# Three moves in a layer of attention and feed-forward, and the scheduler's timeline model for all engines but TensorE

## The chip, the cores and the metric

One core of a Trainium2 chip. The metric is the device time of one execution, in microseconds (us). The engines are called as in the profile: PE is TensorE (PEld its weight loads), DVE VectorE, ACT ScalarE, POOL GpSimd, and SP SyncE, which issues nearly all of the DMAs here.

## The reference

S = 2048 tokens, D = 512, F = 1792; 32 heads of 16; a causal window of 256 tokens. Everything is float32.

```python
def _A_ref(x, wqkv, wo):
    qkv = ...(x @ wqkv).reshape(B, S, 3, H, Dh)...
    q, k, v = qkv[0], qkv[1], qkv[2]
    scores = jnp.einsum("bhqd,bhkd->bhqk", q, k) * (Dh ** -0.5)
    mask = (idx[:, None] - idx[None, :] >= 0) & (idx[:, None] - idx[None, :] < W)
    p = _softmax(jnp.where(mask[None, None], scores, -1e9), axis=-1)
    return ...jnp.einsum("bhqk,bhkd->bhqd", p, v)... @ wo

def _B_ref(x, w1, w3, w2):
    h = _silu(jnp.einsum("bsd,df->bsf", x, w1)) * jnp.einsum("bsd,df->bsf", x, w3)
    return jnp.einsum("bsf,fd->bsd", h, w2)

xn = _layernorm(x, axis=-1)
return x + _A_ref(xn, A_wqkv, A_wo) * _silu(_B_ref(xn, B_w1, B_w3, B_w2))
```

## The kernel before

**Numbers.** Dense products are computed from float16 pairs: an operand is cut into a high half (a cast) and a low half (a subtraction), and a product is three matmuls, high by high, high by low and low by high. That is why so many of the casts and subtractions exist: for each 128x512 operand a cast (mostly on ACT) and one or two subtractions on GpSimd. Weights are also measured (`squares`, L239 on ACT and L241 on DVE, and `measure_down`, L886) and scaled by a power of two before they are cut (`split_pool`, L332, L333 on ACT, L329 on GpSimd).

**Tiles and units.** The tokens are worked in four tiles (t = 0 to 3) of 512. Of attention there are 32 units: four tiles, four groups of eight heads (g), two halves of a group (p). A unit runs `pass1` (scores L650 and their row maxima L664) and `pass2` (scores L730, masks L737, exponentials L740, values L758). Between the batches of a unit `spread` puts pieces of dense work: the projections to Q, K and V (`project`, matmuls L583, evictions L599 on ACT and L603 on DVE; `value`, L553 and L556), the gate and up products (`gate_up`, matmuls L991; tanh L1006 on ACT; product L1010 and L1015 on DVE), the down product, and the outputs (`residual` L1207 and `total` L1222 to L1237).

**Q and K go through DRAM.** They are stored transposed (L606 to L610) to `dQ` and `dK` and read back in another layout as `qa` and `KA` (`fetch`, L626). The reciprocal of the softmax's sums goes through DRAM too (`normalise`: read `dr`, invert it at L799, store and spread it).

**Weights.** Tile 0 loads the raw float32 weights, measures and cuts them. The cut halves of wqkv, w1 and w3 are stored to DRAM (`dWQ` L589, `dW1` L997), and tiles 1 to 3 load them from there (L617, L832). Loads for tile 0 are issued at L384 (wqkv), L836 (w1, w3) and L877 (w2).

**The fold of w2.** Tile 0 multiplies by w2 as it is (L1184). For tiles 1 to 3 the down product is done block by block in seven products in place of eight. That takes sums of blocks of w2, made once, in tile 1's time, by `fold_weights` for seven pairs of blocks: load the raw pair e, o (L943), scale it (ACT, L949), make the sums z and y (GpSimd, L951 to L954), then cut e, o, z and y (`cut`: a cast at L959 on ACT, subtractions at L961 on GpSimd), and store them to `dW2` (L966). On the other side, `fold_first` and `fold_second` make the sums of the hidden activations (GpSimd L1078 to L1081) and cut them (ACT L1053 and L1069; GpSimd L1054, L1072, L1073). `load_fold` (L1095) brings w2's halves back, `fold_down_piece` multiplies (L1114; evictions L1128 on ACT and L1132 on DVE), and `unfold` (L1148) adds the seven results.

**What sets the order.** PE runs in the order in which the program is written (`ORDERED` holds TensorE alone). The instructions of DVE, ACT, GpSimd and SP are ordered by the framework's scheduler, with `urgent()` (a higher priority) around evictions, and `tc.issue_after(x)`, which holds an instruction back behind x. The program's own clock is a count of steps: `later(n, f)` writes f's instructions n steps on. Nearly all operands live in 55 slots of one pool. `give(slot, after=n)` offers a slot for reuse from n steps on; `take` picks the slot that was free earliest:

```python
    def give(*tiles, after=0):
        for made in tiles:
            given[0] += 1
            free.append((now[0] + after, given[0], held.pop(id(made))[0]))
```

An instruction that writes to a reused slot waits for the last reader of what was in it.

Of the kernel before, what the change touches and what calls it, by code (L numbers as in the profile page):

```python
# [21 lines left out]
P = 128  # L22
S = 2048
D = 512
# [22 lines left out]
KR = TERMS * DH  # L47
# [6 lines left out]
ORDERED = {ENGINE.PE}  # L54
# [28 lines left out]
def tile_block(ctx: ExitStack, tc: tile.TileContext, x, wqkv, wo, w1, w3, w2, out):  # L83
# [142 lines left out]
    dW1 = dram.tile([FB, 2, P, 2 * NC * P], F16, name="dW1")  # L226
    dW2 = dram.tile([7, P, FB // 2, D], F16, name="dW2")


    def squares(parts, on_act=0, apart=0):  # L230

# [335 lines left out]
    def project(t, g, k, terms=(range(3),), scores_bank=False):  # L567


        cell = {}  # L570

        parts = ([[(c, i) for c in (2 * half, 2 * half + 1) for i in range(3)] for half in range(2)] if len(terms) == 1
                 else [[(c, i) for i in group for c in range(NC)] for group in terms])

        def part(n):
            assert turned[t] == 4
            w = WQ[t, g, k]
            xh, xl = X[t]
            if n == 0:
                cell["pp"] = pss.tile([P, 2, TW], F32, name="s")[:, 0, :] if scores_bank else bank([P, TW])  # L580
            for c, i in parts[n]:
                a, b = ((0, xh), (1, xh), (0, xl))[i]
                nc.tensor.matmul(cell["pp"], w[:, (a * NC + c) * P:(a * NC + c + 1) * P], b[:, c, :], start=(c, i) == parts[0][0],  # L583
                                 stop=(c, i) == parts[-1][-1])
            if n < len(parts) - 1:
                return
            if t == 0:
                def store():
                    nc.sync.dma_start(dWQ[g, k], w)  # L589
                    give(w, after=4)  # L590
                later(8, store)
            else:
                give(w)
            pp = cell["pp"]
            both = take(F16)
            B = both.rearrange("p (a t) -> p a t", a=2)
            s = QS / (XS * WS)
            with urgent():
                nc.scalar.activation(B[:, 0, :], pp, AF.Copy, scale=s)  # L599

            def rest():
                with urgent():
                    lasts["emptied"] = nc.vector.scalar_tensor_tensor(B[:, 1, :], pp, s, B[:, 0, :], op0=ALU.mult, op1=ALU.subtract)  # L603
                d = (dQ, dK)[k][g][:, :, t * TW:(t + 1) * TW]
                if k == 0:
                    nc.sync.dma_start(d[:, 0:2, :], B[:, 0:1, :].to_broadcast([P, 2, TW]))  # L606
                    nc.sync.dma_start(d[:, 2, :], B[:, 1, :])
                else:
                    nc.sync.dma_start(d[:, 0:2, :], B)
                    nc.sync.dma_start(d[:, 2, :], B[:, 0, :])  # L610
                give(both, after=4)
            later(1, rest)
        return opening([(len(l), lambda n=n: part(n)) for n, l in enumerate(parts)])
# [5 lines left out]
    def fetch(t, g):  # L619
        QA[t, g] = qa = qpool.tile([P, 4, TW], F16, name="qa")  # L620
        ka = keys(t, g)
        c0 = 0 if t else 2 * P
        for dst, d in ((ka[:, :, c0:], dK[g][:, :, t * TW - 2 * P + c0:(t + 1) * TW]),
                       (qa, dQ[g][:, :, t * TW:(t + 1) * TW])):
            for r in range(2):
                nc.sync.dma_start(dst[64 * r:64 * r + KR],  # L626
                                  d[64 * r:64 * r + 64].rearrange("(a d) i t -> (d i) a t", d=DH))


# [197 lines left out]
    def load(t, f):  # L827
        if t:
            a = [take(F16) for _ in range(2)]
            WF[t, f] = [a, None]  # L830
            for k in range(2):
                nc.sync.dma_start(a[k], dW1[f, k])  # L832
            return
        RAW[f] = raw = [take(F32) for _ in range(2)]
        for k, w in enumerate((w1, w3)):
            nc.sync.dma_start(raw[k].rearrange("p (c f) -> p c f", f=P),  # L836
                              w[:, f * P:(f + 1) * P].rearrange("(c p) f -> p c f", p=P))

    measured = set()
# [34 lines left out]

    def load_down(f):
        RAW2[f] = raw = take(F32)
        nc.sync.dma_start(raw, w2[f * P:(f + 1) * P, :])  # L877

    def measure_down(k, f):

# [53 lines left out]
    def fold_weights(j):  # L934

        cell = {}
        l, r = slice(0, 256), slice(256, 512)
        sub = nc.gpsimd.tensor_sub

        def load():  # L940
            cell["raw"] = [take(F32) for _ in range(2)]
            for i, raw in enumerate(cell["raw"]):
                nc.sync.dma_start(raw, w2[(2 * j + i) * P:(2 * j + i + 1) * P, :])  # L943

        def sums():
            assert folded
            e, o = cell["raw"]
            for i, raw in enumerate((e, o)):
                nc.scalar.activation(raw, raw, AF.Copy, scale=fold_w[:, 2 * j + i:2 * j + i + 1])  # L949
            cell["z"] = z, y = [take(F32) for _ in range(2)]  # L950
            sub(z[:, l], e[:, r], e[:, l])  # L951
            sub(z[:, r], o[:, r], z[:, l])
            sub(y[:, l], o[:, r], e[:, r])
            sub(y[:, r], o[:, l], z[:, r])  # L954

        def cut(raw, n, which):

            a = take(F16)
            nc.scalar.copy(a[:, 0:n], raw[:, 0:n])  # L959
            for c in range(0, n, 256):  # L960
                sub(a[:, n + c:n + c + 256], raw[:, c:c + 256], a[:, c:c + 256])  # L961
            give(raw, after=6)

            def store():
                for c, i in enumerate(which):
                    nc.sync.dma_start(dW2[i, :, j, :].rearrange("p (h d) -> p h d", h=2),  # L966
                                      a[:, 0:2 * n].rearrange("p (h c d) -> p c h d", h=2, d=256)[:, c])
                give(a, after=4)
            later(4, store)

        def cuts():
            e, o = cell["raw"]
            z, y = cell["z"]
            for n, work in enumerate(((e, 256, (0,)), (o, 512, (1, 2)), (z, 512, (4, 5)), (y, 512, (6, 3)))):
                later(2 * n, lambda work=work: cut(*work))
        return load, sums, cuts
# [3 lines left out]
    def gate_up(t, f):  # L980
        cell = {}

        def part(k, half):
# [10 lines left out]
                return  # L994
            if t == 0:
                def store():
                    nc.sync.dma_start(dW1[f, k], w)  # L997
                    give(w, after=4)
                later(8, store)
            else:  # L1000
                give(w)
            if k == 0:
                cell["s"] = sg = take(F32)

                with urgent():
                    nc.scalar.activation(sg, cell[0], AF.Tanh, scale=sg_scale[:, f:f + 1])  # L1006

                def product():
                    with urgent():
                        lasts["emptied"] = nc.vector.scalar_tensor_tensor(sg, sg, 1.0, cell[0], op0=ALU.add, op1=ALU.mult)  # L1010
                later(1, product)
            else:
                sg = cell["s"]
                with urgent():
                    lasts["emptied"] = nc.vector.scalar_tensor_tensor(sg, cell[1], 0.5 * HS / (WS * XS)**2, sg,  # L1015
                                                                      op0=ALU.mult, op1=ALU.mult)
                if t:
                    HH[t, f] = sg
                    later(1, lambda: (fold_second if f % 2 else fold_first)(t, f // 2))
                    return  # L1020
                HH[t, f] = hh = take(F16)

                def rest():
                    nc.scalar.copy(hh[:, 0:TW], sg)  # L1024
                    halves(nc.gpsimd.tensor_sub, hh[:, TW:], sg, hh[:, 0:TW])
                    give(sg, after=4)
                later(1, rest)
        return [q for k in range(2) for q in opening([(6, lambda k=k, half=half: part(k, half)) for half in range(2)])]

# [27 lines left out]
    def fold_second(t, j):  # L1057
# [7 lines left out]
        def cut(raw, view, which, give_too=()):  # L1065
# [7 lines left out]
                sub(lo[:, k], view[:, k], hi[:, k])  # L1073
            for k, i in enumerate(which):
                operand(t, j, i, made, 512, 256 * k)
            give(raw, *give_too, after=4)

        nc.gpsimd.tensor_add(z[:, 0], ee[:, 1], oo[:, 1])  # L1078
        sub(z[:, 1], z[:, 0], ee[:, 0])
# [8 lines left out]
    def load_fold(t, k, i):  # L1088

        j0, j1 = FOLDS[k]  # L1090
        WS7[t, k, i] = made = []
        for j in range(j0, j1, 2):
            made.append(take(F16))
            n = min(2, j1 - j)
            nc.sync.dma_start(made[-1].rearrange("p (j d) -> p j d", d=D)[:, 0:n], dW2[i, :, j:j + n, :])  # L1095

    QS7 = {}

# [39 lines left out]
    def unfold(t):  # L1138
# [14 lines left out]
        into(0, 0, q[0], q[1])  # L1153
        halves(add, q[5], q[5], q[4])
        into(0, 1, q[5], q[2])
        give(*q, after=6)
        summed.update((t, b) for b in range(4))

    def folds(t, k):
# [353 lines left out]
    for n in range(len(units)):  # L1513
# [6 lines left out]
                    ahead[n].append((0, lambda k=k, half=half: load_qk(*tiles[k], half)))  # L1520
        if n % 8 >= 4 and t < NT - 1:
            beside[n] += value(4 * t + n % 8)
        if 2 <= n % 8 < 6 and t:
            beside[n] += [(0, lambda t=t, b=n % 8 - 2: residual(t - 1, b))] + total(t - 1, n % 8 - 2)
        beside[n] += ahead[n]
    other = [sum(c for c, _ in b) for b in beside]
    a_unit = (whole - KEEP - EARLY + sum(other)) / len(units)
# [55 lines left out]
```

## Time and profile before

| | us |
|---|---|
| median of 3 runs | 861.5 (861.15 to 862.03) |
| the profiled execution, its own time | 859.68 |
| its span | 857.9 |
| PE busy | 804.5 (94% of the span) |
| DVE busy | 635.0 (74%) |
| POOL busy | 416.1 (49%) |
| ACT busy | 402.1 (47%) |

The mean granted clock of TensorE is 0.982 of full speed. The profile counts an engine as busy while one of its instructions runs; register, branch, semaphore and DMA-issuing instructions are not counted. A row of a group of instructions gives line, engine, operation, output and inputs, shapes and count, then busy time and mean ns of one, then the idle time just before them with what ended it. A matrix product's tile is called m, slot is any of the 55 slots.

### The profile page before, as it was taken

To read this page: it belongs to the slowest core of one execution; us is meant where nothing else is said; L and a number is where in the kernel's file an instruction comes from. 1 tells how busy PE (TensorE), PEld (TensorE's weight loads), DVE (VectorE), ACT (ScalarE), POOL (GpSimd) and SP (SyncE) were. 2 spreads that over 40 slices of the span, in tenths; PEclk is the share of its full clock that TensorE was granted. 3 is DMA by queue.
4 is the path that set the end of the run, shared out by engine and by line. 5 is a ranking of instruction groups with operands and counts; after the bars stand their busy time and mean duration, and the time that the engine had idled before them with its cause. 6 is when DMAs were issued, how large, how long until landed. Compare 5 with 4: busy or idle time off the path is not lost.

```text
span 857.9 us, 24287 instructions
## 1 busy us (share of the span) xinstructions
PE 804.5 (94%) x9302; PEld 420.7 (49%) x9302; DVE 635.0 (74%) x2027; ACT 402.1 (47%) x597; POOL 416.1 (49%) x723
## 2 busy tenths in 40 slices
PE   8998988999999499998999898999999989999997
PEld 4444444444444245654447454456544644457464
DVE  8886796788886378675888777875688778774447
ACT  6899774544565244453443233443444334334411
POOL 2248064341768936346362746421146458551561
PEclk9999999999999799999999999999999999999999
DMA  9999654248356483757554444554545545324411
GB/s 283 259 286 293 197 156 124 90 131 238 90 166 177 113 232 111 231 173 218 163 155 122 152 115 137 144 157 125 160 121 144 138 141 152 109 83 129 127 34 62
DMA packets 118421, 133.82 MB, mean 156 GB/s; under 512 B 19168, under 2 KB 76832, under 8 KB 118304
## 3 DMA queue, kind: packets, MB, share of 16 engines
q1 hardware_dynamic: 118016, 131.74, 52.4%
q8 instruction: 73, 1.20, 0.6%
q10 hardware_dynamic: 288, 0.52, 0.2%
q14 instruction: 44, 0.36, 0.2%
HBM read 94.50 MB, written 33.42 MB: 149 GB/s over the span
## 4 chain that ended last, share of the span: by engine, by line
PE 56%; DVE 14%; POOL 11%; DMA 6%; ACT 5%; issue 4%; SPq 2%; POOLq 0%; ACTq 0%; DVEq 0%
PE m L991 21%; PE m L1114 10%; PE po L758 6%; PE m L583 5%; DVE junk L664 4%; PE m L1228 4%; PE s L730 4%; DMA slot<-in_B_w_dram 3%; POOL slot L329 3%; PE m L553 2%; POOL slot L1073 2%; PE s L650 2%; PE m L1184 2%; DVE s L737 2%; ACT pt L740 1%
## 5 line engine op out<-in xcount | busy, mean ns | idle before, releaser
L991 PE MATMUL m<-XH,slot 128*128 128x512 f16 x896 | 272.9, 387 | 7.5 <-DVE slot L603 4.5
L740 ACT ACTIVATE pt<-s,es 128x1024 f32<-128x1024 f32 x152 | 167.6, 1113 | 157.8 <-DVE s L737 154.7
L991 PEld LDWEIGHTS <-slot 128*128 128x128 f16 x1344 | 126.2, 99 | 166.8 <-issue 28.3
L329 POOL TENSOR_TENSOR slot<-slot,slot 128x256 f16<-128x256 f32 (+1 forms) x156 | 104.2, 697 | 146.0 <-ACT slot L1024 68.2
L991 PE MATMUL m<-XL,slot 128*128 128x512 f16 x448 | 172.5, 385 | 0.0
L737 DVE TENSOR_TENSOR s<-s,MK 128x256 f32<-128x256 f32 (+2 forms) x280 | 119.2, 435 | 57.6 <-PE s L730 54.4
L664 DVE CUSTOM_DVE_ANT_0 junk<-s,MW 128x320 bf16<-128x320 f32 x276 | 134.1, 486 | 20.5 <-PE s L650 11.6
L1114 PE MATMUL m<-slot,slot 128*128 128x256 f16 x882 | 102.7, 273 | 1.9 <-POOL slot L1073 1.2
L1114 PEld LDWEIGHTS <-slot 128*128 128x128 f16 x882 | 84.4, 98 | 19.1 <-issue 5.1
L664 DVE CUSTOM_DVE_ANT_0 junk<-po,MW 128x320 bf16<-128x320 f32 x172 | 83.6, 486 | 5.7 <-DVE al L288 0.5
L583 PE MATMUL m<-XH,slot 128*128 128x512 f16 x240 | 72.4, 386 | 12.8 <-DVE slot L1010 12.8
L1073 POOL TENSOR_TENSOR slot<-slot,slot 128x256 f16<-128x256 f32 x126 | 82.7, 676 | 0.6
L758 PE MATMUL po<-pt,V 64*32 64x320 f32 (+4 forms) x2880 | 77.2, 342 | 0.0
L1010 DVE SCALAR_TENSOR_TENSOR slot<-slot,m 128x512 f32<-128x512 f32 x56 | 38.3, 684 | 43.7 <-ACT slot L1006 43.6
L730 PE MATMUL s<-qa,KA 50*64 50x320 f16 (+3 forms) x1472 | 59.2, 261 | 7.2 <-ACT pt L740 5.0
L583 PEld LDWEIGHTS <-slot 128*128 128x128 f16 x384 | 36.1, 99 | 56.7 <-issue 17.4
L758 PEld LDWEIGHTS po<-pt,V 64*32 64x32 f32 x2880 | 50.3, 106 | 22.3 <-issue 0.8
L730 PEld LDWEIGHTS <-KA 50*64 50x64 f16 x1472 | 31.0, 106 | 58.4 <-issue 38.9
L1078 POOL TENSOR_TENSOR slot<-slot,slot 128x256 f32<-128x256 f32 x21 | 15.3, 728 | 89.4 <-DVE slot L1015 89.4
L1006 ACT ACTIVATE slot<-m,sgs 128x512 f32<-128x512 f32 x56 | 38.2, 682 | 37.9 <-PE m L991 37.8
L329 POOL TENSOR_TENSOR on<-on,rb 128x256 f32<-128x256 f32 x32 | 23.4, 752 | 57.4 <-DMA rb<-de 57.3
L650 PE MATMUL s<-KA,qa 48*64 48x320 f16 (+3 forms) x824 | 45.4, 296 | 4.0 <-ACT pt L740 2.4
(186 smaller groups left out, 1170.7 us busy)
## 6 DMA issues: line engine op xcount, KB each, us to landing
slot<-dW SPq DMA_DIRECT2D x147, 256.0 KB
slot<-in_B_w_dram SPq DMA_DIRECT2D x56, 256.0 KB
slot<-in_A_x_dram SPq DMA_DIRECT2D x30, 256.0 KB
dW<-slot SPq DMA_DIRECT2D x28, 256.0 KB
KA<-dK SPq DMA_DIRECT2D x24, 288.0 KB
dW<-slot SPq DMA_DIRECT2D x49, 128.0 KB
qa<-dQ SPq DMA_DIRECT2D x32, 192.0 KB
slot<-dWQ SPq DMA_DIRECT2D x24, 256.0 KB
```

Source lines behind the costliest of these rows:

```text
L329: op(out[:, c], a[:, c], b[:, c])
L583: nc.tensor.matmul(cell["pp"], w[:, (a * NC + c) * P:(a * NC + c + 1) * P], b[:, c, :], start=(c, i) == parts[0][0], stop=(c, i) == parts[ ...
L650: nc.tensor.matmul(s[c:c + w, r, :n], qa[rows, 2 * p + a, ii * P + c:ii * P + c + w], ka[rows, 2 * p + a, e - n:e], start=True, stop=True)
L664: lasts["maximum"] = nc.vector.tensor_tensor_reduce(out=junk[:, :n], in0=s[:, r, :n], in1=mask, scale=1.0, scalar=NEG, op0=ALU.add, op1=AL ...
L730: nc.tensor.matmul(s[64 * h:64 * h + 64, r, o:o + 64 * n], ka[rows, 2 * p + a, 64 * (m + 4):64 * (m + 5)], qa[rows, 2 * p + a, 64 * (m + k ...
L737: nc.vector.tensor_add(v, v, MK[:, kind, of:of + n, :].unsqueeze(1).to_broadcast([P, 2 * len(which), n, 64]))
L740: nc.scalar.activation(pt, s, AF.Exp, scale=es)
L758: nc.tensor.matmul(cell["po"][32 * i:32 * i + 32, h, 64 * (m + k):64 * (m + k + n)], V[64 * h:64 * h + 64, (4 * t + m // 2) % VB, hd * VW: ...
L991: nc.tensor.matmul(cell[k], w[:, (a * NC + c) * P:(a * NC + c + 1) * P], b[:, c, :], start=c == 0 and i == 0, stop=c == NC - 1 and i == 2)
L1010: lasts["emptied"] = nc.vector.scalar_tensor_tensor(sg, sg, 1.0, cell[0], op0=ALU.add, op1=ALU.mult)
L1073: sub(lo[:, k], view[:, k], hi[:, k])
L1114: nc.tensor.matmul(ps, made[:, f:f + P], wj[:, 256 * b:256 * b + 256], start=j == j0 and n == 0, stop=j == j1 - 1 and n == 2)
```

## The change

1. In `fold_weights`, the casts of the sums z and y go from ACT (14 casts of 128x512) to GpSimd (28 casts of 128x256). Those of e and o stay on ACT.
2. Slots are offered for reuse later: 14 steps rather than 6 in `fold_weights`, 8 rather than 4 in `gate_up`, 14 rather than 4 in `fold_second`, 16 rather than 6 in `unfold`.
3. For tiles 1 and 2's outputs (written during tiles 2 and 3), `residual` and `total` are written one unit later.
4. The stores of cut weights to `dWQ`, `dW1` and `dW2` are held behind the load that was written last on SP (`behind_load`).
5. The scheduler orders DVE, ACT, GpSimd and SP by its model of the timeline (`schedule_with_timeline_sim=True`). PE's order stays written by hand; units and pieces are the same, but for the outputs of point 3.

```diff
+    def behind_load():
+
+        return tc.issue_after(lasts["load"].ins) if "load" in lasts else nullcontext()
+
...
                 def store():
-                    nc.sync.dma_start(dWQ[g, k], w)
+                    with behind_load():
+                        nc.sync.dma_start(dWQ[g, k], w)
                     give(w, after=4)
...
-                nc.sync.dma_start(dst[64 * r:64 * r + KR],
+                lasts["load"] = nc.sync.dma_start(dst[64 * r:64 * r + KR],
...
-                nc.sync.dma_start(a[k], dW1[f, k])
+                lasts["load"] = nc.sync.dma_start(a[k], dW1[f, k])
...
-            nc.sync.dma_start(raw[k].rearrange("p (c f) -> p c f", f=P),
+            lasts["load"] = nc.sync.dma_start(raw[k].rearrange("p (c f) -> p c f", f=P),
...
-        nc.sync.dma_start(raw, w2[f * P:(f + 1) * P, :])
+        lasts["load"] = nc.sync.dma_start(raw, w2[f * P:(f + 1) * P, :])
...
             a = take(F16)
-            nc.scalar.copy(a[:, 0:n], raw[:, 0:n])
+            if any(raw is r for r in cell["raw"]):
+                nc.scalar.copy(a[:, 0:n], raw[:, 0:n])
             for c in range(0, n, 256):
+                if not any(raw is r for r in cell["raw"]):
+                    nc.gpsimd.tensor_copy(a[:, c:c + 256], raw[:, c:c + 256])
                 sub(a[:, n + c:n + c + 256], raw[:, c:c + 256], a[:, c:c + 256])
-            give(raw, after=6)
+            give(raw, after=14)
 
             def store():
                 for c, i in enumerate(which):
-                    nc.sync.dma_start(dW2[i, :, j, :].rearrange("p (h d) -> p h d", h=2),
-                                      a[:, 0:2 * n].rearrange("p (h c d) -> p c h d", h=2, d=256)[:, c])
+                    with behind_load():
+                        nc.sync.dma_start(dW2[i, :, j, :].rearrange("p (h d) -> p h d", h=2),
+                                          a[:, 0:2 * n].rearrange("p (h c d) -> p c h d", h=2, d=256)[:, c])
...
-                    nc.sync.dma_start(dW1[f, k], w)
+                    with behind_load():
+                        nc.sync.dma_start(dW1[f, k], w)
...
                     halves(nc.gpsimd.tensor_sub, hh[:, TW:], sg, hh[:, 0:TW])
-                    give(sg, after=4)
+                    give(sg, after=8)
...
-            give(raw, *give_too, after=4)
+            give(raw, *give_too, after=14)
...
-            nc.sync.dma_start(made[-1].rearrange("p (j d) -> p j d", d=D)[:, 0:n], dW2[i, :, j:j + n, :])
+            lasts["load"] = nc.sync.dma_start(made[-1].rearrange("p (j d) -> p j d", d=D)[:, 0:n], dW2[i, :, j:j + n, :])
...
-        give(*q, after=6)
+        give(*q, after=16)
...
-        if 2 <= n % 8 < 6 and t:
-            beside[n] += [(0, lambda t=t, b=n % 8 - 2: residual(t - 1, b))] + total(t - 1, n % 8 - 2)
+        b = n % 8 - (2 if t == 1 else 3)
+        if 0 <= b < 4 and t:
+            beside[n] += [(0, lambda t=t, b=b: residual(t - 1, b))] + total(t - 1, b)
...
-    with _tile.TileContext(nc) as tc, tc.manual_schedule(engines=ORDERED):
+    with _tile.TileContext(nc, schedule_with_timeline_sim=True) as tc, tc.manual_schedule(engines=ORDERED):
```

## The prediction

> **What bounds the kernel now.** I read the page first, for the shares of the engines:
>
> ```profile
> span 857.9 us, 24287 instructions
> PE 804.5 (94%) x9302; PEld 420.7 (49%) x9302; DVE 635.0 (74%) x2027; ACT 402.1 (47%) x597; POOL 416.1 (49%) x723
> ```
>
> TensorE is busy for 804.5 of 857.9 us. Its order is written by hand and stays, so the change can move only its idle time, and the time it spends at a lower clock. Where that lies, the view by windows tells. Its columns are the window, its length, then busy time (instructions) of PE, PE's weight loads, DVE, ACT and POOL, the granted clock, the DMA share and GB/s:
>
> ```profile
> 0.00:25.00 25.00, 22.81 (x107) 10.60 (x108) 21.18 (x68) 16.99 (x29) 5.35 (x33) 1.00 0.98 282
> 25.00:50.00 25.00, 24.45 (x180) 10.80 (x178) 18.52 (x83) 20.76 (x47) 9.51 (x14) 1.00 1.04 277
> 50.00:175.00 125.00, 111.24 (x1189) 52.84 (x1188) 96.35 (x368) 92.37 (x172) 60.14 (x102) 0.99 0.60 182
> 225.00:250.00 25.00, 23.23 (x306) 11.46 (x303) 22.57 (x73) 10.53 (x16) 15.19 (x25) 1.00 0.43 131
> 250.00:275.00 25.00, 22.92 (x274) 11.19 (x267) 16.37 (x50) 15.46 (x26) 20.35 (x34) 0.93 0.57 166
> 275.00:300.00 25.00, 13.97 (x180) 6.33 (x179) 10.28 (x31) 9.02 (x14) 24.62 (x41) 0.80 0.46 128
> 375.00:400.00 25.00, 22.66 (x262) 10.52 (x261) 19.17 (x58) 11.03 (x16) 19.02 (x32) 0.97 0.59 184
> 475.00:550.00 75.00, 68.51 (x757) 32.48 (x757) 55.98 (x164) 27.48 (x35) 37.85 (x64) 0.95 0.47 132
> 675.00:700.00 25.00, 22.97 (x311) 15.39 (x309) 19.41 (x56) 7.86 (x9) 11.17 (x16) 1.00 0.66 180
> 725.00:775.00 50.00, 47.89 (x580) 24.30 (x578) 37.30 (x119) 19.28 (x24) 27.64 (x48) 0.97 0.37 114
> ```
>
> Three stages lose differently. Up to 50 us TensorE is nearly full, and the DMA engines are at their limit (share 0.98 and 1.04, 282 and 277 GB/s). From 275 to 300 GpSimd is busy for 24.62 of 25 us and TensorE for 13.97. After that come smaller holes. The view of waits names who waits for whom (total, times, longest), and the chain of the fold's window shows the large hole (start, length):
>
> ```profile
> PE m L583 <- DVE slot L1010: 12.8, 4, 11.0
> ACT slot L959 <- POOL slot L1073: 14.4, 3, 9.0
> ACT slot L1222 <- POOL slot L1073: 6.6, 2, 4.1
> DVE dr L799 <- DMA dr<-dd: 13.7, 7, 3.8
> ```
>
> ```profile
> 262.82 3.90 DMA slot<-in_B_w_dram
> ...
> 289.66 3.76 POOL slot L961 x6
> 293.43 0.69 POOL slot L952
> ...
> 294.67 0.69 ACT slot L1006
> 295.38 0.70 DVE slot L1010
> ```
>
> So the hole of 11.0 us is one queue of GpSimd work: ACT's cast of a sum (L959) waits for GpSimd's subtraction (L952), the tanh L1006 stands behind that cast on ACT, the product L1010 behind the tanh, and the projection's matmul L583 behind the bank which L1010 empties.
>
> **The change, part by part.** All against the profiled execution, 859.68 us with a span of 857.9.
>
> *Early transfers.* This part of the diff is only the new scheduler, and it is the dear one. The queue of SP today, and its reader:
>
> ```profile
> 14.37 2.70 SPq L836 DMA_DIRECT2D slot<-in_B_w_dram  x4
> 18.93 0.34 SPq L610 DMA_DIRECT2D dK<-slot  x1
> ...
> 22.99 0.38 SPq L610 DMA_DIRECT2D dK<-slot  x1
> 24.76 0.81 SPq L626 DMA_DIRECT2D KA<-dK  x2
> 25.66 0.88 SPq L626 DMA_DIRECT2D qa<-dQ  x2
> ```
>
> ```profile
> 29.74 0.24 PE L650 MATMUL s<-KA,qa 48*64 48x128 f16 x1 [0.18 <-DMA qa<-dQ]
> ```
>
> TensorE's first scores (L650) already wait for the read of Q (0.18 us). In the compiled order of before, the last DMA of that first read-back (L626) is the 34th on SP, with 6.96 MiB up to it. In the changed order it is the 51st, with 11.09 MiB: fifteen loads of weights for later steps (two of wqkv, eight of w1 and w3, five of w2) and the next group's stores now stand ahead of it, and one store of dWQ no longer does. That is 4.13 MiB, or 4.33 MB, and at 0.28 MB per us (282 and 277 GB/s above) 15.5 us. SP had holes before the read-back, 17.07 to 18.93 and 23.37 to 24.76, 3.2 us together. Loads can fill these, but the DMA share of 0.98 says that the engines had a backlog meanwhile, so I take off 2.0: **+13.5** (10 to 17). TensorE has nothing else to do then, as its order is fixed.
>
> The idle time also costs clock. After the 11.03 us hole the first matmuls run long:
>
> ```profile
> 296.12 1.01 PE L583 MATMUL m<-XH,slot 128*128 128x512 f16 x2 [11.03 <-DVE slot L1010]
> ...
> 300.49 0.59 PE L583 MATMUL m<-XH,slot 128*128 128x512 f16 x2
> ```
>
> 0.42 us more for two, for some three such pairs: **+1.3** (0 to 3).
>
> *Early ACT order.* In the changed order about ten squares of weights (L239, L886) that wait for those late loads stand ahead of evictions that TensorE needs (L556, L1006). The groups' rows (busy, mean ns, idle before) price this and the next parts:
>
> ```profile
> L239 ACT ACTIVATE sqa<-slot 128x512 bf16<-128x512 f32 x34 | 21.4, 628 | 4.9 <-DMA slot<-in_B_w_dram 3.1 <-DMA slot<-in_A_wqkv_dram 1.2
> L949 ACT ACTIVATE slot<-slot,fw 128x512 f32<-128x512 f32 x14 | 9.7, 717 | 6.4 <-DMA slot<-in_B_w_dram 6.4
> L1072 POOL CAST slot<-slot 128x256 f16<-128x256 f32 x84 | 32.5, 401 | 21.0 <-issue 9.4 <-PE m L1228 5.4 <-PE m L1114 5.2
> ```
>
> Ten by 0.628 is 6.3 us if none is covered; as TensorE holds two banks, I take half, **+3.1** (0 to 6.3). On the other hand, what ACT, GpSimd and the loads do during the stall is done when today's holes come: from 50 to 175 us TensorE idles 125 − 111.24 = 13.8 us, from 225 to 250 1.8 us, and 0.01 of the clock over 125 us is 1.2 us. I take half of these 16.8 us back, **−8** (−3 to −13). Near 195 us, five scalings of w2 (L949) now stand ahead of an exponential that TensorE reads: 5 × 0.717 = 3.6, of which I take **+2.5** (0 to 4).
>
> *w2's fold, 250 to 300 us.* Taking 14 casts from ACT frees it from waiting on GpSimd's sums, so the path quoted goes. Gone are 11.0 us and its 1.3 of clock, 2.1 us of idle time from 250 to 275 and 0.07 × 25 = 1.8 of clock there: 16.2. (The 0.80 of the last window counts clock granted while idle; I price that by the matmuls.) Next in line is GpSimd itself. It gets 28 casts of 128x256; the nearest row is L1072 of the same shape, 28 × 0.401 = 11.2 us. In 250 to 300 it has 4.65 + 0.38 = 5.0 us free, so 6.2 us are late, unless they slip into the free 9.8 us of the window before; and L949 now stands 0 to 1.4 us of work behind its load's issue, where a load took 3.90 us: some 1.3. Together 7.5, net **−8.7** (−15 to −2).
>
> *After 300 us.* The slots given back later (8, 14, 16 steps), the outputs one unit later and the stores behind the last load serve the same waits. The rings of waiting are GpSimd's cuts (L1073), then an output's tanh that reuses the slot (L1222), then DVE, then TensorE. In the changed order no such pair stands close. The idle time in the four quoted windows is 2.3 + 6.5 + 2.0 + 2.1 = 13.0 us, and the clock 0.03 × 25 + 0.05 × 75 + 0.03 × 50 = 6.0: 19.0 in all. But the reciprocal L799, which waits for a round trip through DRAM, now stands earlier in DVE's order in 15 of 16 groups, and what is queued behind it are evictions. Seven waits cost DVE 13.7 today, 2.0 each; nine more cost 17.6, and with DVE idle a quarter of the time I let half reach TensorE, 9: net **−10** (−18 to −2). The stores and later slots by themselves add nothing on an engine; the cover is the free DMA time (shares of 0.37 to 0.66), and if slots ran short, loads would come late by the 3.90 us above.
>
> Does a short hole cost clock?
>
> ```profile
> 748.86 0.42 PE L730 MATMUL s<-qa,KA 50*64 50x320 f16 x12 [1.63 <-DVE M L664]
> 749.69 0.42 PE L730 MATMUL s<-qa,KA 50*64 50x320 f16 x12 [0.41 <-ACT pt L740]
> ...
> 750.30 1.03 PE L991 MATMUL m<-XH,slot 128*128 128x512 f16 x2
> ```
>
> After 1.63 us of idle time a pair takes 1.03 us as against 0.59, so it does here. [...]
>
> *Sum:* 13.5 + 1.3 + 3.1 − 8 + 2.5 − 8.7 − 10 = −6.3, so 853.4 for the profiled execution. The median of the runs, 861.5, is 1.0021 times that execution's 859.68, which gives **855**.
>
> **The rivals.**
> 1. *The early stall decides (slower).* Place: the first L650. The read-back waits 17 us, the ten squares cost their full 6.3, and only 3 us come back later, since the holes after 100 us have other causes than late loads. Sum 17 + 1.3 + 6.3 − 3 + 2.5 − 8.7 − 10 = +5.4, and 867. It decides once the early terms pass the 18.7 of gains; in my sum they are 12.4. For it speak the saturated DMA rows; against it, that half of the early holes do follow late weights.
> 2. *No early stall (much faster).* If the small read-backs are served beside the queued loads, 13.5 + 1.3 go: −21.1, and 840. Against it: the wait on qa at 29.74 shows a read taking 3 us and more in that traffic. [...]
> 3. *GpSimd stays the bound of the fold.* With 24.62 of 25 us taken and 11.2 added, tile one's operands come as late as today, and the fold saves nothing: −6.3 + 8.7 = +2.4, and 864.
>
> That the scheduler changes nothing is excluded: the orders of SP and GpSimd differ widely.
>
> **How the numbers follow.** Forecast 0.45, first rival 0.26, second 0.12, third 0.17. A measurement of this kernel tells 0.2%, 1.7 us, from no change. The forecast's bounds reach both sides: faster in 0.8 of it, the same in 0.12, slower in the rest; the first rival is nearly all slower, the second all faster, the third 0.04 faster, 0.04 the same, 0.09 slower. That makes 0.53, 0.11 and 0.36. The range, 842 to 870, holds the forecast's spread (843 to 864), the third rival and most of the first; it leaves out most of the second and the end of the first.
>
> **What would show it.** Right: the first L650 stands after 40 us, with 10 us or more of idle before it; ACT's casts no longer wait on L1073, the hole before L583 near 285 is under 5 us, and the windows after 300 lose half their idle time. Wrong: L650 starts by 32 us (second rival); TensorE's idle time from 50 to 175 stays near 13.8 (first rival); a hole above 8 us behind GpSimd between 250 and 320 (third rival); or new holes after 300 behind L799 above 13 us in all, which no case here has.

## The result, and the profile after

The changed kernel takes 902.7 us (median of 3, 897.4 to 904.9) against 861.5: the ratio is 1.048, 95% interval 1.046 to 1.051. The forecast was 855 us, with a range from 842 to 870. The profiled execution took 904.90 us. In the experiments below one of the four runs of fix_dve_sp (905.9 us; the others took 891.5 to 895.4) is a slow one and left out of its time, but its trace is of that run. Here is the page of the profiled execution, and with it the windows up to 300 us that were shown of before (same columns), and one behind them that got worse:

```profile
span 903.1 us, 24317 instructions
PE 818.0 (91%) x9302; PEld 426.3 (47%) x9302; DVE 646.1 (72%) x2027; ACT 394.7 (44%) x583; POOL 423.0 (47%) x751
```

```profile
0.00:25.00 25.00, 21.74 (x104) 10.15 (x105) 19.96 (x66) 15.83 (x27) 5.33 (x33) 1.00 1.01 283
25.00:50.00 25.00, 12.18 (x53) 4.97 (x53) 7.85 (x32) 19.97 (x50) 5.05 (x8) 0.73 1.09 288
50.00:175.00 125.00, 110.40 (x1097) 51.55 (x1095) 91.58 (x360) 80.42 (x148) 53.39 (x90) 0.96 0.54 164
225.00:250.00 25.00, 21.34 (x232) 9.71 (x231) 17.44 (x63) 12.66 (x19) 12.02 (x20) 0.93 0.45 107
250.00:275.00 25.00, 21.75 (x280) 10.78 (x278) 20.24 (x67) 8.45 (x12) 10.05 (x17) 1.00 0.18 51
275.00:300.00 25.00, 18.12 (x215) 9.05 (x215) 20.14 (x48) 10.83 (x17) 21.23 (x38) 0.90 0.40 112
300.00:375.00 75.00, 62.55 (x626) 28.26 (x621) 50.55 (x138) 30.58 (x43) 52.46 (x90) 0.87 0.60 171
```

TensorE's busy time grew by 13.5 us on the same matmuls, which goes with the lower clock (a mean of 0.964 as against 0.982; 0.73 from 25 to 50, 0.87 from 300 to 375), and its idle time by 31.7. The hole of 11.0 us at the fold is gone. One of 11.5 at the first scores and eleven others above 2 us, up to 6.9, have come; before there were four others, up to 3.8. The view of waits (total, times, longest):

```profile
PE s L735 <- DVE mt L694: 17.2, 7, 6.9
PE s L655 <- DMA qa<-dQ: 12.4, 2, 11.5
PE m L587 <- DVE slot L1020: 9.1, 4, 4.7
DVE dr L804 <- DMA dr<-dd: 39.7, 15, 6.8
ACT slot L954 <- DMA slot<-in_B_w_dram: 17.9, 8, 5.2
```

Lines have moved by a few: L650 is now L655, L664 L669, L799 and L800 are L804 and L805, L949 is L954, L1010 L1020. The reciprocal waits for its round trip in 15 of 16 groups, 39.7 us in all; before, it was 7 times and 13.7 us.

Where the time goes can be read by following one instruction that both kernels have: the row maxima on DVE (512 in each). By how much the changed kernel starts the same maximum later:

| maximum (start before, us) | 31 | 42 | 205 | 246 | 360 | 530 | 771 |
|---|---|---|---|---|---|---|---|
| later after the change, us | 13.0 | 16.8 | 22.6 | 29.8 | 41.7 | 51.8 | 46.2 |

So 17 us are lost in the first 42 us, 6 more by 205, 19 from there to 360 (7 of them by 246, 12 in the time of w2's fold), and 10 by 530; then 6 come back.

**The start.** SP issues thirteen loads one behind the other, more of them between the stores of K and Q, and the first read-back of these comes behind all:

```profile
14.13 3.27 SPq L841 DMA_DIRECT2D slot<-in_B_w_dram  x4
17.45 1.90 SPq L388 DMA_DIRECT2D slot<-in_A_wqkv_dram  x2
19.40 4.04 SPq L841 DMA_DIRECT2D slot<-in_B_w_dram  x4
23.48 2.61 SPq L882 DMA_DIRECT2D slot<-in_B_w_dram  x3
...
35.42 0.85 SPq L631 DMA_DIRECT2D KA<-dK  x2
36.38 0.89 SPq L631 DMA_DIRECT2D qa<-dQ  x2
```

```profile
42.09 0.31 PE L655 MATMUL s<-KA,qa 48*64 48x128 f16 x1 [11.53 <-DMA qa<-dQ]
...
43.88 0.61 PE L557 MATMUL m<-wvh,XH 128*128 128x512 f16 x1
```

The read-back of Q issues at 36.4 rather than 25.7 us, and the first scores wait 11.5 us and then 0.9. A single matmul then takes 0.61 us (0.38 before the hole), and 0.63 up to 48.5 us; the granted clock from 42 to 46 us was 0.50.

**The fold.** Here a row shows something that no trace of before had. Three views: DVE, GpSimd and TensorE near 290 us.

```profile
289.94 0.35 DVE L804 RECIPROCAL dr<-dr 128x32 f32<-128x32 f32 x1 [2.85 <-DMA dr<-dd]
290.33 7.11 DVE L805 TENSOR_SCALAR dr<-dr,so 128x32 f32<-128x32 f32 x1
297.36 0.42 DVE L742 TENSOR_TENSOR s<-s,MK 128x256 f32<-128x256 f32 x1
...
317.37 6.23 DVE L681 TENSOR_SCALAR NM<-M 128x16 f16<-128x16 f32 x1
```

```profile
288.04 3.80 POOL L969 TENSOR_TENSOR slot<-slot,slot 128x256 f16<-128x256 f32 x6
291.80 0.71 POOL L1088 TENSOR_TENSOR slot<-slot,slot 128x256 f32<-128x256 f32 x1
...
296.38 0.39 POOL L1082 CAST slot<-slot 128x256 f16<-128x256 f32 x1
296.74 0.66 POOL L1083 TENSOR_TENSOR slot<-slot,slot 128x256 f16<-128x256 f32 x1
```

```profile
299.17 0.64 PE L735 MATMUL s<-qa,KA 50*64 50x320 f16 x8 [6.88 <-DVE mt L694]
```

The scaling of the reciprocal, 128x32, usually takes 0.24 us. Here it takes 7.11 us, and ends when GpSimd's unbroken run of work ends (296.74 + 0.66 = 297.40). Everything on DVE stands behind it, and TensorE idles 6.9 us. The same happens at 317.37: L681, 128x16, takes 6.23 us in place of 0.17, until a run of GpSimd ends at 323.56, and TensorE idles 4.7 us before L587. Both stand on the chain of work that ended last (the first is called issue there), with a load of w2 between them for which ACT's scaling L954 waits:

```profile
290.37 6.99 issue
...
305.56 4.12 DMA slot<-in_B_w_dram
309.79 0.73 ACT slot L954
...
317.37 6.24 DVE NM L681
```

### The profile page after: what moved, and what is told of

It reads as the page before. It is cut to its first block, busy times and chain, and to the rows that moved or that the text cites. A ratio compares the mean times of both kernels' runs of the same rounds, so it can differ in the third digit from the quotient of the medians.

```text
span 903.1 us, 24317 instructions
## 1 busy us (share of the span) xinstructions
PE 818.0 (91%) x9302; PEld 426.3 (47%) x9302; DVE 646.1 (72%) x2027; ACT 394.7 (44%) x583; POOL 423.0 (47%) x751
## 4 chain that ended last, share of the span: by engine, by line
PE 47%; DVE 17%; DMA 15%; ACT 6%; SPq 6%; issue 5%; POOL 4%; DVEq 0%; ACTq 0%; POOLq 0%
PE m L1000 16%; PE m L1124 7%; PE po L763 5%; DVE junk L669 5%; DMA slot<-in_B_w_dram 4%; SPq L785 4%; DMA dr<-dd 4%; PE m L1238 4%; PE m L587 3%; PE m L557 3%; PE s L735 3%; PE m L1194 3%; DMA dd<-os 2%; DVE s L742 2%; DMA dW<-slot 2%
## 5 line engine op out<-in xcount | busy, mean ns | idle before, releaser
L333 POOL TENSOR_TENSOR slot<-slot,slot 128x256 f16<-128x256 f32 (+1 forms) x156 | 102.9, 691 | 168.7 <-ACT slot L1034 76.4
L669 DVE CUSTOM_DVE_ANT_0 junk<-s,MW 128x320 bf16<-128x320 f32 x276 | 133.6, 484 | 22.6 <-PE s L655 13.3
L669 DVE CUSTOM_DVE_ANT_0 junk<-po,MW 128x320 bf16<-128x320 f32 x172 | 83.5, 486 | 5.3
L587 PE MATMUL m<-XH,slot 128*128 128x512 f16 x240 | 73.6, 391 | 9.3 <-DVE slot L1020 9.1
L1020 DVE SCALAR_TENSOR_TENSOR slot<-slot,m 128x512 f32<-128x512 f32 x56 | 38.4, 685 | 41.4 <-ACT slot L1016 37.1
L655 PE MATMUL s<-KA,qa 48*64 48x320 f16 (+3 forms) x824 | 46.4, 299 | 23.6 <-DMA qa<-dQ 12.4
L333 POOL TENSOR_TENSOR on<-on,rb 128x256 f32<-128x256 f32 x32 | 22.8, 733 | 90.9 <-DMA rb<-de 90.5
L587 PEld LDWEIGHTS <-slot 128*128 128x128 f16 x384 | 36.2, 100 | 54.4 <-issue 15.1
L655 PEld LDWEIGHTS <-qa 48*64 48x64 f16 (+1 forms) x1200 | 31.7, 103 | 51.7 <-issue 23.6
```

The lines of the kernel that those rows point to most:

```text
L333: op(out[:, c], a[:, c], b[:, c])
L655: nc.tensor.matmul(s[c:c + w, r, :n], qa[rows, 2 * p + a, ii * P + c:ii * P + c + w], ka[rows, 2 * p + a, e - n:e], start=True, stop=True)
L669: lasts["maximum"] = nc.vector.tensor_tensor_reduce(out=junk[:, :n], in0=s[:, r, :n], in1=mask, scale=1.0, scalar=NEG, op0=ALU.add, op1=AL ...
```

## The experiments

All in one table (the median in us, and the ratio to the kernel before, run beside it on the same chip, with its 95% interval):

| run | us | ratio |
|---|---|---|
| timeline_only | 890.9 | 1.036 (1.030 to 1.042) |
| moves_only | 861.0 | 0.999 (0.997 to 1.001) |
| reads_first | 898.3 | 1.043 (1.039 to 1.046) |
| late_reciprocal | 886.2 | 1.029 (1.026 to 1.031) |
| free_stores_moves | 867.3 | 1.005 (1.003 to 1.007) |
| free_stores | 901.9 | 1.047 (1.042 to 1.053) |
| act_held | 897.5 | 1.041 (1.035 to 1.047) |
| all_held | 877.6 | 1.017 (1.013 to 1.021) |
| fix_dve | 885.8 | 1.028 (1.021 to 1.035) |
| fix_sp | 892.9 | 1.035 (1.028 to 1.041) |
| fix_act | 903.8 | 1.047 (1.041 to 1.054) |
| fix_pool | 896.6 | 1.039 (1.032 to 1.047) |
| fix_dve_sp | 892.3 | 1.039 (1.036 to 1.043) |
| fix_dve_sp_pool | 883.2 | 1.032 (1.025 to 1.038) |
| fix_act_sp | 891.8 | 1.034 (1.030 to 1.038) |
| casts_only | 864.3 | 1.004 (1.002 to 1.007) |
| slots_outputs | 860.7 | 1.002 (0.999 to 1.004) |
| outputs_only | 855.9 | 0.994 (0.992 to 0.996) |

**The scheduler alone, and the moves alone.** In timeline_only the last line of the diff is applied to the kernel before; in moves_only everything but it.

```diff
-    with _tile.TileContext(nc) as tc, tc.manual_schedule(engines=ORDERED):
+    with _tile.TileContext(nc, schedule_with_timeline_sim=True) as tc, tc.manual_schedule(engines=ORDERED):
```

> The kernel before with the timeline model and none of the four moves. If the model's order is what costs (theory): about 900 us (890 to 912), with the 12 us stall at the first L650 and DVE waiting some 40 us for dr before the reciprocal. If the moves cost (rival): 861 to 870 us, with DVE's wait on dr near the 13.7 us of before.

> The changed kernel without the timeline model: the four moves alone. Theory: as fast as before or faster, 845 to 862 us, the hole of 11 us near 285 us gone or under 5. Rival (the moves cost, above all the casts on GpSimd): 880 us or more, with GpSimd full from 250 to 320 us.

Both times fall into the theory's range: the order costs 29 us by itself, the moves are worth nothing by themselves (0.999), and together they lose 12 us more than the one alone. In timeline_only DVE waits 33.4 us for dr, in all 16 groups, and the first scores 13.9 us. For moves_only the theory fails on the hole, which was to be gone or under 5 us: one of 9.7 us ends at 306. Followed by the row maxima, moves_only loses 12 us between 306 and 343 us and wins 13 between 463 and 771. In the view by time of ACT, what stands before this hole is a cast that waits for a slot which a store still reads:

```profile
304.85 0.41 ACT L965 CAST slot<-slot 128x256 f16<-128x256 f32 x1 [13.29 <-DMA dW<-slot]
```

**Reads ahead of the loads.** Each load of raw weights is queued behind the read-back written last.

```diff
+            with behind_read():   # tc.issue_after(lasts["read"].ins), set in fetch
                 lasts["load"] = nc.sync.dma_start(raw[k]..., w[...])
```

> The changed kernel with every load of raw weights held behind the read-back of K and Q that was written last, so that the fifteen loads issue behind the first reads again. Theory (the loads ahead of the read-back cost 13 us there and some 4 more in the unit behind it): 886 us (881 to 891), the first L650 at 30 to 32 us. Rival (the time is only put off, since the weights then come later and TensorE waits for them): 897 us or more.

The rival holds, mostly. The first scores come at 31 us, and yet the kernel gains only 4 us: at the maximum that stood at 78 us it is 12 us behind the kernel before again. ACT's view by time suggests why (the line numbers of this kernel are some seven higher): the tanh L1023, for which TensorE waits 5.0 us, stands behind squares that wait for loads.

```profile
47.67 0.63 ACT L898 ACTIVATE sqa<-slot 128x512 bf16<-128x512 f32 x1 [2.37 <-DMA slot<-in_B_w_dram]
...
57.48 0.67 ACT L1023 ACTIVATE slot<-m,sgs 128x512 f32<-128x512 f32 x1
```

**A later reciprocal.**

```diff
+            with tc.issue_after(lasts["maximum"].ins):
                 nc.vector.reciprocal(dr, dr)
                 nc.vector.tensor_scalar(dr, dr, sc["o"], None, op0=ALU.mult)
```

> The changed kernel with the reciprocal L804 and the scaling behind it held behind the row maximum that was written last on DVE, which puts it some 16 us of TensorE's work behind the copies L778 rather than some 10. Theory (DVE's queue stands still behind the reciprocal for 39.7 us in all, and TensorE's holes next to it make 26 us and some clock): 876 us (868 to 886), DVE's wait on dr under 8 us. Rival (another wait takes its place at once): 895 us or more.

It brings 16.5 us, the most that holding back one kind of instruction brings, and DVE's wait on dr falls from 39.7 us to this:

```profile
DVE dr L805 <- DMA dr<-dd: 7.8, 3, 6.1
```

26 were expected. By the row maxima (the two profiled executions are 19.8 us apart) 11 us are won by 343 and 8 behind it. Some comes back: the product with the reciprocals (L333) waits on GpSimd 10.55 us for them at 468 us, and behind it stand small steps of the next tile's layer norm that DVE needs, so TensorE has a hole of 9.0 us, where the changed kernel has one of 5.3.

**Stores free again.** w2's stores to dW2 are not held behind loads, once without and once with the timeline model.

```diff
-                    with behind_load():
-                        nc.sync.dma_start(dW2[i, :, j, :]...
+                    nc.sync.dma_start(dW2[i, :, j, :]...
```

> The four moves without the timeline model, and w2's stores to dW2 no longer held behind a load. Theory (in the run of the moves alone ACT's cast L965 waited 13.3 us for a store to free its slot, and a hole of 9.7 us of TensorE stood behind it): 848 us (844 to 853), that hole under 3 us. Rival (the hole is GpSimd's load, now with 28 more casts, and the store only came last): 857 us or more.

> The changed kernel, timeline model included, with w2's stores to dW2 not held behind a load. Theory (the 12 us by which the changed kernel is slower than the timeline model alone are these stores): 892 us (887 to 897). Rival (the 12 us are the slots and outputs under the model's order): 900 us or more.

The theory fails in both, and the rivals' times hold. Without the hold, the kernel of the moves gets 6 us slower. The chain at its hole of 8.3 us now runs through GpSimd's cuts and casts to the same cast on ACT and the tanh behind it, so the store was only what came last (why the kernel gets slower stays open):

```profile
300.44 1.30 POOL slot L969 x2
301.76 0.62 ACT slot L965
302.38 0.60 ACT slot L1015
```

With the timeline model the stores make no difference that these runs can tell. Which of the other moves makes the 12 us under the model's order no run shows.

**Squares behind evictions; everything held.**

```diff
+                with behind_eviction():   # tc.issue_after(lasts["act"].ins), set at L560, L604, L745, L1016
                     nc.scalar.activation(sq, raw, AF.Square, accum_out=ssq[:, i:i + 1])
```

> The changed kernel with the reads first (as in the run of that name, 898 us), and ACT's squares of weights and scalings of w2 (L243, L891, L954) held behind the eviction that was written last on ACT. Theory (with the reads first the time was only put off, because squares that wait for late loads stand ahead of evictions on ACT): 886 us (881 to 891), and TensorE's holes at 40 and 54 us, 8.5 us together, under 3. Rival (the late weights themselves, whatever the order on ACT): 895 us or more.

> The changed kernel with all four held at once: reads first, squares and scalings behind evictions, the reciprocal behind a row maximum (some 10 to 13 us of TensorE's work behind the copies L778, not 16), w2's stores not held behind loads. Theory (the model's order costs where an instruction waits for a DMA in front of others, and nowhere else): 863 us (855 to 871). Rival (its order is worse elsewhere too): 878 us or more.

act_held gains nothing, so the rival holds, and the squares' order by itself is not shown to be the cause. The holes at 40 and 54 us shrink from 8.5 to 6.1, since a square held behind one eviction still stands ahead of the next; a new one of 5.0 us ends at 86.5, where TensorE waits for the sums of squares that were held back; and DVE's scaling by the reciprocals takes 12.3 us beside GpSimd. In all_held the reciprocal is also written four steps earlier than in late_reciprocal. The four together bring 25 us, not 40: the rival on the model's order holds. In its trace, too, such a scaling takes 10.0 us at 277.

**One engine's order put back.** The numbers of the traced instructions of some engines, in the order that they have in moves_only, are written into the program and chained; the timeline model orders the rest.

```diff
+        fixed_order(nc, tc)   # for each two neighbours in the list: tc.add_manual_dep(i, prev.name, NoSync)
```

> The changed kernel, with DVE's instructions held in the very order that they have in the kernel of the moves alone; the timeline model orders ACT, GpSimd and SP round that. Of 42 us (903 against 861) the theory gives DVE's order the largest share, as the reciprocal held late by itself brought 16.5: 884 us (877 to 890). Rival (the other engines' orders then set TensorE's holes): 897 us or more.

> The changed kernel, with SP's DMAs in the very order of the kernel of the moves alone; the other engines as the timeline model orders them round that. Theory (the early stall of 12.4 us and the slow unit behind it are SP's order, and holding the reads alone only failed because it also held the weights too far back): 888 us (882 to 894). Rival (ACT stands still for the late weights as before): 897 us or more.

> The changed kernel, with ACT's instructions in the very order of the kernel of the moves alone; the other engines as the timeline model orders them round that. Theory (squares, scalings and casts of w2 stand in front of evictions in the model's order; they wait 42 us for DMAs, a part of it on TensorE's path): 893 us (886 to 898). Rival (these waits are hidden): 901 us or more.

> The changed kernel, with GpSimd's instructions in the very order of the kernel of the moves alone; the other engines as the timeline model orders them round that. Theory (GpSimd has no share in the 42 us): 902 us (897 to 907). Rival (the fold's operands are late by its order): 895 us or less.

DVE's order put back brings 17 us, SP's 10, GpSimd's 6 (barely clear of the spread), ACT's none by itself. The theories hold for DVE and SP and the rival for ACT; GpSimd's time lies just between theory and rival. Followed by the row maxima, in us behind moves_only:

| maximum (start in moves_only) | 31 | 99 | 208 | 249 | 376 | 541 | 774 |
|---|---|---|---|---|---|---|---|
| changed kernel | 13.1 | 20.0 | 19.3 | 26.9 | 26.1 | 41.4 | 43.6 |
| SP put back | 0.9 | 12.3 | 12.2 | 16.7 | 18.7 | 23.4 | 25.6 |
| ACT put back | 12.5 | 12.6 | 11.7 | 12.5 | 29.4 | 39.5 | 42.2 |
| DVE put back | 12.6 | 19.9 | 19.1 | 26.1 | 15.0 | 21.7 | 19.6 |
| GpSimd put back | 12.9 | 20.1 | 20.9 | 27.3 | 15.7 | 24.2 | 28.8 |
| ACT and SP put back | 0.4 | -1.2 | -4.0 | 1.2 | 12.4 | 24.8 | 27.2 |
| DVE, SP and GpSimd put back | 0.3 | 13.3 | 16.0 | 22.9 | 17.4 | 19.8 | 19.3 |

The start is SP's and ACT's; the gain of DVE's and of GpSimd's order comes at the fold and behind it. ACT's order put back wins 7 to 14 us up to 249 and loses them at the fold, where its trace has three small DVE operations of 5.2 to 9.7 us. One thing has to be kept in mind here: moves_only itself loses 12 us at the fold, so the changed kernel, which is no further behind it at 376 than at 249, loses 12 there against the kernel before as well.

> The changed kernel with ACT's and SP's orders both held as in the kernel of the moves alone; DVE and GpSimd by the timeline model. Theory (the loss of 19 us in the first 100 us is made by these two, each enough for 12 by itself): by the unit at 100 us no more than 3 us behind the moves alone, and 880 us in all (874 to 886), the rest being DVE's reciprocals. Rival (DVE's and GpSimd's orders hold the start up too): 10 us or more behind by 100 us, 890 us or more.

The part on the start holds: with both put back the kernel is 1.2 us ahead of moves_only at 99 us, where each alone leaves 12 us. The total does not: 892, against 880. From 249 to 376 it loses 11 us, and small DVE operations stand still for 28 us in all, more than in any other run:

```profile
255.21 9.73 DVE L681 TENSOR_SCALAR NM<-M 128x16 f16<-128x16 f32 x1
```

```profile
291.49 10.02 DVE L681 TENSOR_SCALAR NM<-M 128x16 f16<-128x16 f32 x1
```

TensorE's next scores wait 7.8 us behind the first, and L587 8.4 us behind the second. Over all traces: in each of the runs with GpSimd's order made by the timeline model one to four of the 48 operations of these two kinds (128x32 and 128x16) take 2.4 to 12.3 us. With GpSimd's order from moves_only (fix_pool, fix_dve_sp_pool), and in the kernel before, moves_only, outputs_only and casts_only, none takes over 0.8; slots_outputs has one of 3.3 and free_stores_moves one of 1.6.

> The changed kernel with DVE's and SP's orders both held as in the kernel of the moves alone; ACT and GpSimd by the timeline model. Alone they brought 16.9 and 9.8 us. Theory (two separate costs, the reciprocals on DVE and the early stall on SP): 876 us (870 to 881). Rival (they share a cost, each wait covering the other): 881 to 886.

> As the run before, and GpSimd's order held too, so that ACT alone follows the timeline model. Theory (ACT's order costs some 8 us in the first 100 us, where squares stand in front of evictions, and little behind it): 869 us (864 to 874). Rival (with the other three in place ACT's order costs nothing): 861, give or take 2.

Both miss: the gains do not add. DVE and SP together (892) are worse than DVE alone (886), and with ACT alone left to the model 883 us stand where 861 to 869 was expected. So the one order of ACT, which was worth nothing against the changed kernel, costs 22 us against the moves, all of it by 249 us (last row of the table). Its waits there are the loads, in front of everything else on ACT:

```profile
ACT sqa L891 <- DMA slot<-in_B_w_dram: 16.1, 5, 6.9
ACT slot L954 <- DMA slot<-in_B_w_dram: 16.0, 5, 8.0
```

**Single moves.** On the kernel before, without the timeline model: the casts alone, the later slots (not the fold's) with the later outputs, and the outputs alone. The edits are those of the diff.

> The kernel before with one move alone: the casts of w2's sums on GpSimd. Theory (GpSimd is full from 266 to 300 us, 28 casts of some 0.4 us add 11 us to its queue): 870 us (866 to 874), the hole near 285 us longer than 11. Rival (ACT, rid of its waits on GpSimd, gives the time back, as the prediction had it): 855 us or less.

> The kernel before with only two of the moves: later reuse of slots (all but the one in the fold of w2) and later outputs; no casts on GpSimd, no stores behind loads, no timeline model. Theory (the moves alone lose 12 us at the fold, from the casts and the held stores, and win 12 us behind it, from these two): 850 us (846 to 855). Rival (the gain behind the fold is only time that the delay at the fold handed on): 858 to 863.

> The kernel before with one move alone: the outputs of tiles 1 and 2 one unit later. Nothing in it differs before some 420 us, so the fold keeps its hole of 11 us. Theory (of the gain of 12 us that the moves show behind 480 us this move is the larger part, as GpSimd's cuts have a unit more before an output reuses their slots): 852 us (848 to 856). Rival (the gain was only time that the delay at the fold handed on): 858 to 862.

casts_only lies between theory and rival: 4 us slower (1.004), its hole near 285 still 9.1 us (the row below), and a new one of 1.9 at 308. The 28 casts measured 0.397 us each, 11.1 in all, so the price was right and more than half of it is hidden. slots_outputs is the same as before, as its rival had it, its fold hole 10.5 and a new one of 5.8 us at 306. outputs_only is faster, 0.994, as the theory had it: the one version that beats both kernels, at 855.9 us.

```profile
PE m L583 <- DVE slot L1013: 10.8, 4, 9.1
```

The windows of outputs_only, to be read beside those of before in the prediction:

```profile
275.00:300.00 25.00, 13.99 (x181) 6.34 (x180) 10.30 (x31) 9.02 (x14) 24.62 (x41) 0.80 0.44 127
...
475.00:550.00 75.00, 70.21 (x871) 34.43 (x870) 56.85 (x172) 27.36 (x34) 45.40 (x78) 0.95 0.49 140
675.00:700.00 25.00, 24.39 (x320) 15.80 (x318) 20.30 (x59) 7.36 (x8) 13.27 (x21) 1.00 0.59 164
725.00:775.00 50.00, 48.45 (x632) 26.89 (x639) 38.35 (x120) 20.58 (x25) 25.74 (x43) 1.00 0.38 116
```

The hole at the fold is untouched; TensorE's idle time falls from 6.5 to 4.8, from 2.0 to 0.6 and from 2.1 to 1.6 us, and the clock rises in the last window from 0.97 to 1.00.

## Why the prediction was wrong

Its sum was −6.3; the profiled executions differ by +45.2. By stretches, 12.4 was forecast and 22.6 measured up to 205 us, −8.7 and +19.2 from there to 360, −10 and +4.5 up to 771. The steps in order:

- *Early transfers, +13.5: right.* 11.5 + 0.9 us of waits at the first scores, less the 0.5 of before, are 11.9. Q's read-back stood behind the loads on SP: it issued at 36.4 us rather than 25.7, and the first scores waited 11.5 us for it, so here the small reads were not served beside the queued loads. The second rival falls with it.
- *Clock after it, +1.3: too small.* The unit behind the hole is 3.8 us longer with no idle time in it. I had priced three pairs of matmuls; the slow ones go on, at 0.61 to 0.63 us each.
- *ACT's order +3.1 and the return of −8: wrong, the first step that failed.* From 42 to 205 us the kernel did not win 4.9 but lost 5.8: the idle time of TensorE that was to be won back rose from 13.7 to 17.6 us on the same work. ACT did work ahead during the stall, on squares, without a wait between 27 and 44 us; from 56 us on its squares wait for loads again, ahead of the tanh that TensorE needs. fix_sp shows that this order costs 12 us even where the stall is gone, and fix_act_sp that with it and SP's put back nothing is left. So the loss of the first 100 us, 20 us, has two causes that cover each other in part, each good for 12.
- *The fold, −8.7: wrong, by far the largest miss.* From 205 to 360 us the kernel lost 19. What makes the 7 up to 246 stays open (in the table, ACT put back loses 0.8 from 208 to 249, ACT and SP put back 5.2). The path that I removed did go: no cast of a sum waits for L952 on ACT. But I costed GpSimd's fuller queue as lateness of its own results alone, 6.2 us. What I did not see is that small DVE operations would stand still until a run of GpSimd's ended: 6.9 and 6.1 us of it in the two operations above, both on the chain, with holes of 6.9 and 4.7 us behind them and a granted clock of 0.50 from 299 to 303 and from 326.6 to 330 us. The runs are not longer than before (15.4 and 17.4 us, against one of 17.9 from 280.7). fix_pool, which has no such operation, and fix_dve, which has one of 5.6 us, are each 10 to 11 us less behind at 376 us. That the stalls make the whole loss is not shown: moves_only, which has none, loses 12 us here as well, with holes of 9.7 and 6.6, and timeline_only, without the moves, loses 8, with one operation of 10.9 us. So the moves were no gain at the fold under either scheduler. The rest I can't divide with certainty; ACT waits 17.9 us in all for the loads of L954, and DVE for dr.
- *After 360, −10: wrong sign up to 530, right behind it.* 10 us are lost to 530, then 6 won. The reciprocal was named as the danger and its wait under-sized: 26.0 us more on DVE against 17.6. late_reciprocal gives 16.5 us for holding it back, more than half of it by the end of the fold; for all of it I had taken 9.
- *The moves as gains: wrong.* In moves_only they lose 12 us at the fold and win as much behind it. The casts alone cost 4 us and the outputs alone win 5; I had put the later slots down at nothing, and slots_outputs, whose fold is 11 us behind by 343 us, shows that, but for those of the fold, they cost about what the outputs bring. Part of the 13 us won behind the fold is then only its delay handed back.

The first rival was the right one in place and sign, at 867, and too cheap. Its early terms, 24.1, come near the 22.6 measured by 205, in part by luck, as its stall of 17 was 11.9; behind them it kept −8.7 and −10 like the forecast, and these failed. Of the signs that were named, L650's start (42.1 us, 11.5 idle before it) and the hole before L583 (now 4.7) came out as for right, and TensorE's idle time from 50 to 175, 14.6, as for the first rival. What I read off the orders (loads ahead of reads, squares ahead of evictions, reciprocals earlier) was there; the weight that I gave to the gains was not supported by any row that showed an engine's order to be better elsewhere. What stays open: why the fold takes back what ACT's order put back wins before it, so that this order costs nothing in one setting and 22 us in the other, and what the model assumes of a DMA's duration, which no run here shows.

## What to carry to other kernels

An order for several queues is one thing made of all of them. Here an instruction that waited for a DMA kept what stood behind it in its queue waiting too: 17.9 us in all on ACT for loads (L954), 39.7 us in all on DVE for round trips (`dr`), and in moves_only 13.3 us on ACT for a slot that a store still read. Putting it later in its queue paid only as far as its own reader allowed: it brought 16.5 us for the reciprocal (whose reader on GpSimd once waited 10.55 us), 4 for the reads, and nothing for the squares. Before trusting a scheduler's order, list which DMA waits stand at the head of each queue, and sum what is queued behind them; gains from undoing single ones overlapped here (DVE's and SP's orders brought 17 and 10 us alone, 10 together), so measure pairs. A change made of several moves should be run move by move: here one of them alone beat both kernels.

## What the runs showed of the hardware that was not expected

Small DVE operations stood still until GpSimd paused: 7.11 us for a 128x32 scaling and 6.23 us for a 128x16 one in the changed kernel, up to 12.26 us in act_held. Each of these three begins while GpSimd is at work and ends 0.03 to 0.04 us behind the end of a GpSimd instruction after which GpSimd does nothing for 5.9 us or more; over all traces the pause behind those above 2.3 us is 1.4 us or more. During the two in the changed kernel parts of thirteen and of twelve GpSimd instructions ran. What stops DVE there no run shows. It is not so in every run of GpSimd's: in the kernel before, 28 of the 48 operations begin while GpSimd is at work, and all end within 0.8 us, at the end of one instruction or two. It is not the length of the run: in the kernel of the moves alone one begins at 285.64 inside an unbroken run of 17.8 us and takes 0.71 us. What tells the two kinds of run apart stays open.
